# Pooled attention with two MLPs: products with v of two key tiles in one TensorE task, in all pairs of heads

## The chip, the cores and the metric

The kernel runs on one core of one Trainium2 chip. The metric is the device time of one execution in microseconds (us), the median of several runs. TensorE is called PE here, VectorE DVE, ScalarE ACT, GpSimd POOL, and SyncE, whose queue issues all DMAs of this kernel, SP.

## What is computed

```python
# q, k, v: (2, 8, 1152, 64); 16 heads in all
q_pool = q.reshape(B, H, S // 2, 2, D).mean(axis=3)        # 576 pooled queries a head
scores = (1 / sqrt(D)) * q_pool @ k.transpose(0, 1, 3, 2)  # 576 x 1152
attn = softmax(scores, axis=-1)
x = (attn @ v)  -> (1152 tokens, 512)
h = x @ moe_w_in;  x = maximum(0.01 * h, h) @ moe_w_out    # 512 -> 2048 -> 512
h = x @ moe2_w_in; out = (h * sigmoid(h)) @ moe2_w_out
```

## The kernel before, in words

**Tiling.** Attention works on 8 pairs of heads, one after the other, numbered p = 0 to 7. The two heads of a pair (j = 0, 1) share the partitions, 64 rows each. The keys lie in 9 tiles of 128 (t = 0 to 8). For each head and key tile, `scores` makes 128 keys x 576 queries in two halves of 288 columns: per half two matmuls at L675, the second one adding the low part of q and the negated row maximum, and then ACT takes the exponential at L679 into a tile `e` in SBUF. A ring holds ten such tiles, five key tiles of both heads. The row maxima of a pair are found one pair ahead: `max_tile` makes 27 groups a pair of scores on PE (L586; L582 and L583 for the rows left over), and DVE reduces each at L590. Scores and maxima take turns in six PSUM banks; two more banks belong to the product with v.

**The products.** `pv` (L701) multiplies the `e` tiles of a key tile with v. A step is four matmuls at L712: two halves of 288 columns, and in each the two heads, whose outputs lie on partitions 0 to 63 and 64 to 127. They stand in F32, so the trace shows two records for each matmul, 8 for a step. All 9 steps of a pair accumulate in the same two banks; ACT then copies these out (`evac_pv`, L727).

**The rest of a pair.** POOL adds the `e` tiles up over the keys (`sum_up`, L696, 16 adds a pair, on DVE in the last pair). When the 16th is done, PE sums them over the partitions (`sums`, L741), and small DMAs bring the reciprocals into shape (DVE L776). DVE and ACT scale and split the result (`finish`, L816 to L820). For a later pair, POOL pools q (L480), ACT and DVE split q and k into a high and a low part (L350, L499, L504), and DMAs on SP move these where PE wants them. In the later pairs, the first weights of the MLPs are loaded and split too, the low part on POOL (L169).

**What sets the order.** All work is put down as tasks of a `Plan`, each with an engine, a weight (its assumed time), a due time, what it comes after, and tokens that it takes and gives (banks, tiles). `Plan.run` goes through a model of time: an engine that is free takes the ready task with the earliest due time, and the instructions are written out in the order in which the tasks begin there. So the due time and the weight of one kind of task can move the instructions of all engines. On the chip each engine then works in the order written, and waits by semaphores. A `pv` task has the weight 0.25 + 0.98 for each key tile in it.

**The loop around the change.** For each pair, `attention` puts down the scores and exponentials of all key tiles, the adds, and then a task `pv` for each entry of a list of groups of key tiles; the task comes after all exponentials of its group, and is due by its last key tile. The list of groups for the last pair stands in `PARAMS`:

```python
    last_pv=((0, 1), (2, 3), (4, 5), (6, 7), (8,)),
```

The MLPs follow attention, with a plan of their own. Their lines are L1080 (first matrix), L1151 and L1200 (second).

Of the kernel before, what the change touches and what calls it, by code (L numbers as in the profile page):

```python
# [18 lines left out]
def pooled_attention_two_mlps(  # L19
# [27 lines left out]
    t=26.5,  # L47
# [10 lines left out]
    last_pv=((0, 1), (2, 3), (4, 5), (6, 7), (8,)),  # L58
# [227 lines left out]
def attention(ctx, tc, q, k, v, xh, xl, weights, end_p):  # L286
# [4 lines left out]
    NKT = S // 128  # L291
# [4 lines left out]
    NP = B * H // 2  # L296
# [7 lines left out]
    P = PARAMS  # L304
# [101 lines left out]
    def load_v(p, due):  # L406
        b, h0 = p // HP, 2 * (p % HP)

        def go():
            vnat[p] = nat.tile([128, 2, NKT, D], F32, tag="vnat", name="vnat")  # L410
            return vnat[p], v[b, h0:h0 + 2].rearrange("j (p t) d -> p j t d", p=128)

        return dma(due, go, take=("vnat",), lag=6.0, begin=due)
# [139 lines left out]
    def copy_ka(p, j, out, due, after):  # L553
        if p == 0:
            parts = (slice(0, 512), slice(512, S))
            for i, cs in enumerate(parts):
                go = lambda cs=cs: (KA[p % 2, j][own[j], cs].bitcast(F32), K2[p, j][own[j], cs].bitcast(F32))
                out["ka", j, i] = [dma(due, go, after=out["kh", j, i] + after, lag=3.0)]
        else:
            go = lambda: (KA[p % 2, j][own[j]].bitcast(F32), K2[p, j][own[j]].bitcast(F32))  # L560
            out["ka", j, 0] = out["ka", j, 1] = [dma(due, go, after=out["kh", j, 0] + after, lag=P["lag"] + 1.0)]
# [34 lines left out]
    def max_unit(u2, out, due, after):  # L596

        p = 0
        j, u = divmod(u2, NFULL + 1)
        deps = []  # L600
        for i in (0, 1) if u == NFULL else (j,):
            deps += out["qu", i][0 if u < 2 else 1] + out["k", i, 0] + out["k", i, 1]

        def pe():
            i = box["trio", u2] = trios.pop(0)
            ps = psum[:, i:i + 3].rearrange("p b n -> p (b n)")
            for c in range(0, S, 512):
                ks = slice(c, min(c + 512, S))
                for h, cs, rows in ((1, slice(SQ - 128, SQ), 128), (0, slice(NFC, SQ), HALF)) if u == NFULL else ((j, slice(u * 128, (u + 1) * 128), 128),):
                    nc.tensor.matmul(out=ps[0:rows, ks], lhsT=QH[p, h][:, cs], rhs=K2[p, h][:, ks], start=True, stop=True)  # L610

        def dve():
            i = box.pop(("trio", u2))
            ps = psum[:, i:i + 3].rearrange("p b n -> p (b n)")
            nc.vector.tensor_reduce(out=max_row(p, j)[:, u:u + 1], in_=ps[:, 0:S], op=ALU.max, axis=AX.X, negate=True)
            (trios.append if u2 < 2 * NFULL - 1 else lambda i: banks.extend(range(i, i + 3)))(i)

        t = add("PE", 1.05 if u == NFULL else 0.53, due, pe, after=deps, take=("trio",))
        t = add("DVE", 1.37, due - 1.0, dve, after=[t], give=("trio",) if u2 < 2 * NFULL - 1 else ("bank",) * 3)
        finish_rows(p, j, [u], t, out, due, after)  # L620
# [224 lines left out]
    for p in range(NP):  # L845
        at = lambda x: T0 + (p + x) * T
        out = {}
        due = 0.0 if p == 0 else P["load1"] if p == 1 else at(P["load"])
        loads = load_kq(p, due, due)
        value = load_v(p, at(-0.6) if p else P["load0"])  # L850
        if p == 0:
            for j in range(2):
                prep_first(p, j, loads, out)
        else:
            prep(p, loads, P["prep1"] if p == 1 else [at(x) for x in P["prep"]], out)
        for j in range(2):
            copy_ka(p, j, out, at(-0.5) if p else 5.0 + 2 * j, scored.get((p - 2, j), []) + (filled[p] if p < 2 else []))
        maxima = {}
        for u in range(2 * NFULL + 1 if p == 0 else 0):
            max_unit(u, out, 1.0 + 1.4 * u, filled[0])  # L860
        for n in range(NM if p else 0):
            lo, hi = P["max"]
            due = at(lo + (hi - lo) * n / NM)
            j, u = n // NA, n % NA // NCH
            maxima.setdefault((j, u), []).append(max_tile(p, n, out, due))
        for j in range(2 if p else 0):
            after = scored.get((p - 3, j), []) + (filled[p] if p < 3 else [])
            us = list(range(NFULL + 1 - j))
            finish_max(p, j, us, sum((maxima[j, u] for u in us), []), out, at(-0.2), after)
        ex, av = {}, {}  # L870
        steps = [(t, j) for t in range(NKT) for j in range(2)]
        if p == 0:
            steps = [(t, 0) for t in range(P["lead"])]
            for t in range(NKT):
                steps += [(t, 1)] + [(t + P["lead"], 0)] * (t + P["lead"] < NKT)
        for i, (t, j) in enumerate(steps):
            due = at(i / (2 * NKT))
            ex[t, j], before = scores(p, t, j, out, due, before)
            if t == 1:
                av[t, j] = sum_up(p, t, j, ex[0, j] + ex[1, j], [av[1, 0]] if j else [], due + 2.0)  # L880
            elif t > 1:
                av[t, j] = sum_up(p, t, j, ex[t, j] + [av[t - 1, j]], [], due + 2.0)
        if p == 0:
            add("-", 0.0, 0.0, after=[x for t in range(P["lead"]) for x in ex[t, 0]], give=("v",))
        last = []
        for ts in P["last_pv"] if p == NP - 1 else [(t,) for t in range(NKT)]:
            after = [x for t in ts for j in range(2) for x in ex[t, j]] + ([] if ts[0] else [value])
            x = pv(p, ts, at((2 * ts[-1] + 1) / (2 * NKT)) + P["pv"], after, last)
            last = [x]
            for t in ts:  # L890
                for j in range(2):
                    add("-", 0.0, 0.0, lambda t=t, j=j, p=p: e_t.pop((p, j, t)), after=[x, av[max(t, 1), j]], give=(("e", p, t, j),))
        for j in range(2):
            scored[p, j] = ex[NKT - 1, j]
        add("-", 0.0, 0.0, after=scored[p, 0] + scored[p, 1], give=("ops",))
        values = evac_pv(p, last[0], at(1.0) + 1.0)
        ends = [av[NKT - 1, 0], av[NKT - 1, 1]]
        if p < NP - 1:
            finish(p, sums(p, ends, at(P["sums"])) + values, at(P["norm"] + 0.3 * (p == NP - 2)))
# [396 lines left out]
```

## Time and profile before

| | |
|---|---|
| median of 3 runs | 666.66 us (666.63 to 666.75) |
| span of the profiled execution, first to last instruction | 664.7 us |
| its own time | not listed apart; the median of the runs lies 2.0 us above the span |
| PE busy | 646.1 us, 97% of the span |
| POOL busy, DVE busy, ACT busy | 392.0, 441.3, 326.8 us |
| attention (up to the first L1080 matmul) | 259.4 us |

A busy share is a mean over stages. Matmuls are pipelined and the records of two neighbours overlap, so what a matmul costs is read from one start to the next start, not from its length. Where an engine waits, the row says so in brackets, with the engine that released it.

### The profile page before, as it was taken

The numbers are of one execution on the slowest core, as the hardware profiler recorded it, in microseconds if no ns is written. First come the engines' busy times: TensorE is split into PE (matmuls) and PEld (weight loads), VectorE is DVE, ScalarE is ACT, GpSimd is POOL, SyncE is SP. The second block draws the span as 40 slices with busy tenths as digits, with TensorE's granted clock in tenths as the row PEclk, the third lists the DMA queues.
The fourth block names the chain that finished last, engine by engine and source line by source line (L and its number), as shares of the span: only waits on it lengthen the run. The fifth ranks groups of instructions, "written<-read, shape, count | busy, mean of one in ns | idle before, by whom it ended". The sixth has DMA issues, their size and how long they took to land.

```text
span 664.7 us, 9922 instructions
## 1 busy us (share of the span) xinstructions
PE 646.1 (97%) x3616; PEld 534.6 (80%) x3616; DVE 441.3 (66%) x614; ACT 326.8 (49%) x661; POOL 392.0 (59%) x278
## 2 busy tenths in 40 slices
PE   4889999999999998999999999999999999999997
PEld 3666777777777766988988988999988998888986
DVE  7284756678878766875676676698988888522222
ACT  4655766758686566554533433355456534312110
POOL 8657888897999833644544544476656453522120
PEclk9789999999999999999999999999999999999999
DMA  8636455455944130132233223232233322000012
GB/s 213 139 107 149 126 152 145 116 163 136 263 120 135 52 97 19 63 101 92 94 95 96 96 96 95 96 96 76 83 96 128 103 88 96 0 1 1 0 48 95
DMA packets 27959, 65.87 MB, mean 99 GB/s; under 512 B 9324, under 2 KB 9352, under 8 KB 27912
## 3 DMA queue, kind: packets, MB, share of 16 engines
q1 hardware_dynamic: 27912, 65.26, 33.7%
q8 instruction: 28, 0.46, 0.3%
q14 instruction: 19, 0.16, 0.1%
HBM read 49.81 MB, written 2.42 MB: 79 GB/s over the span
## 4 chain that ended last, share of the span: by engine, by line
PE 93%; POOL 2%; DMA 1%; ACT 1%; DVE 1%; issue 1%; SPq 0%; ACTq 0%; POOLq 0%; DVEq 0%
PE ph L1080 30%; PE po L1151 15%; PE pf L1200 15%; PE psum L675 12%; PE psum L712 11%; PE psum L586 7%; DMA k<-e 1%; PE psum L741 1%; DMA knat<-in_k_dram 1%; PE psum L583 1%; PE psum L582 1%; POOL k L439 0%; POOL e L504 0%; ACT qh L350 0%; ACT k L350 0%
## 5 line engine op out<-in xcount | busy, mean ns | idle before, releaser
L1133 POOL TENSOR_TENSOR gl<-a,gh 128x512 fp32r<-128x512 f32 (+1 forms) x64 | 97.3, 1520 | 143.1 <-ACT gh L1127 76.4
L696 POOL TENSOR_TENSOR acc<-acc,e 128x576 f32<-128x576 f32 x98 | 147.4, 1529 | 24.2 <-ACT e L679 23.8
L590 DVE TENSOR_REDUCE mx<-psum 128x1 f32<-128x384 f32 x189 | 96.5, 550 | 61.9 <-PE psum L586 55.7
L679 ACT ACTIVATE e<-psum 128x288 f32<-128x288 f32 x288 | 101.3, 414 | 69.8 <-PE psum L675 52.0
L1080 PE MATMUL ph<-xh,w0h 128*128 128x320 f32 (+1 forms) x384 | 109.0, 338 | 1.7 <-ACT pvs L727 1.7
L1080 PE MATMUL ph<-xl,w0h 128*128 128x320 f32 (+1 forms) x384 | 108.7, 337 | 0.0
L1080 PE MATMUL ph<-xh,w0l 128*128 128x320 f32 (+1 forms) x384 | 108.7, 337 | 0.0
L675 PE MATMUL psum<-qh,k 128*128 128x288 f32 x288 | 88.3, 323 | 1.7 <-ACT e L679 1.7
L712 PE MATMUL psum<-e,vnat 128*64 128x288 f32 x576 | 85.9, 423 | 0.0
L675 PE MATMUL psum<-ql,ka 128*128 128x288 f32 x288 | 81.8, 300 | 0.5 <-DMA ql<-mn 0.5
L675 PEld LDWEIGHTS psum<-qh,k 128*128 128x128 f32 x288 | 56.4, 196 | 26.3 <-issue 13.6
L1080 PEld LDWEIGHTS ph<-xh,w0h 128*128 128x128 f32 x384 | 67.7, 188 | 9.3 <-ACT pvs L727 2.2
L134 DVE TENSOR_SCALAR wt<-wt 128x512 f32<-128x512 f32 x56 | 40.3, 720 | 50.0 <-ACT wt L130 50.0
L1080 PEld LDWEIGHTS ph<-xh,w0l 128*128 128x128 f32 x384 | 66.9, 188 | 5.6
L1080 PEld LDWEIGHTS ph<-xl,w0h 128*128 128x128 f32 x384 | 66.9, 188 | 5.0
L169 POOL TENSOR_TENSOR w1l<-wt,w1h 128x512 fp32r<-128x512 f32 x32 | 44.4, 1398 | 39.1 <-ACT w1h L165 39.1
L586 PE MATMUL psum<-k,qh 128*128 128x384 f32 x168 | 62.8, 442 | 1.8 <-DMA k<-e 1.4
L169 POOL TENSOR_TENSOR w0l<-wt,w0h 128x512 fp32r<-128x512 f32 x32 | 44.7, 1396 | 24.3 <-ACT w0h L165 24.3
L138 DVE TENSOR_SCALAR wt<-wt 128x512 uint32<-128x512 uint32 x56 | 57.8, 1033 | 1.6
L712 PEld LDWEIGHTS psum<-e,vnat 128*64 128x64 f32 x576 | 35.8, 138 | 27.3 <-issue 12.0
L586 PEld LDWEIGHTS psum<-k,qh 128*128 128x128 f32 x168 | 47.1, 318 | 12.5 <-issue 4.9
L1106 ACT ACTIVATE gh<-ph 128x512 fp32r<-128x512 f32 (+1 forms) x32 | 20.9, 652 | 72.6 <-PE ph L1080 72.6
(89 smaller groups left out, 1162.8 us busy)
## 6 DMA issues: line engine op xcount, KB each, us to landing
wraw<-in_moe_w_in_dram SPq DMA_DIRECT2D x32, 512.0 KB, 3.9
wraw<-in_moe_w_out_dram SPq DMA_DIRECT2D x32, 512.0 KB, 3.3
vnat<-in_v_dram SPq DMA_DIRECT2D x8, 576.0 KB, 4.2
ka<-k SPq DMA_DIRECT2D x14, 288.0 KB, 5.2
knat<-in_k_dram SPq DMA_DIRECT2D x6, 576.0 KB, 6.0
qnat<-in_q_dram SPq DMA_DIRECT2D x6, 576.0 KB, 4.9
k<-knat SPq DMA_DIRECT2D x12, 288.0 KB, 3.3
out_dram<-acc SPq DMA_DIRECT2D x9, 256.0 KB, 2.0
```

The source lines that it names most:

```text
L138: nc.vector.tensor_scalar(out=t, in0=t, scalar1=4, scalar2=1, op0=ALU.logical_shift_left, op1=ALU.logical_shift_right)
L169: self.nc.gpsimd.tensor_tensor(out=lo, in0=tf, in1=hi, op=ALU.subtract)
L586: nc.tensor.matmul(out=ps[:, 0:KC], lhsT=QH[p, j][:, t:NFC:NFULL], rhs=K2[p, j][:, ks], start=True, stop=True)
L590: nc.vector.tensor_reduce(out=mx[p][:, n:n + 1], in_=ps[:, 0:KC], op=ALU.max, axis=AX.X)
L675: nc.tensor.matmul(out=ps[:, 0:C], lhsT=lhsT[:, ks], rhs=rhs[:, cs], start=not last, stop=last)
L679: nc.scalar.activation(out=e_t[p, j, t][:, cs], in_=ps[:, 0:C], func=ACTF.Exp, scale=scale)
L696: e.tensor_tensor(out=acc[p, j], in0=e_t[p, j, 0] if t == 1 else acc[p, j], in1=e_t[p, j, t], op=ALU.add)
L712: nc.tensor.matmul(out=vps[p, c][own[j], 0:C], lhsT=vnat[p][:, j, t, :], rhs=e_t[p, j, t][:, c * C:(c + 1) * C], start=(t == 0), stop=(t = ...
L1080: nc.tensor.matmul(out=box[x][:, c, 0:n], lhsT=wt[:, kk, fs], rhs=m[:, kk, chunk(g, c)], start=(kk == 0 and wt is wh and m is xh), stop=(k ...
L1133: nc.gpsimd.tensor_tensor(out=gl, in0=box["a", x], in1=gh, op=ALU.subtract)
L1151: nc.tensor.matmul(out=box[x][:, c, 0:n], lhsT=wt[:, f, ms], rhs=y[:, c * n:(c + 1) * n], start=(f == 0 and wt is oh and y is gh), stop=(f ...
L1200: nc.tensor.matmul(out=box[x][:, 0, :], lhsT=y[:, ts], rhs=wt[:, f, :], start=(f == 0 and y is gh and wt is oh), stop=(f == FB - 1 and y i ...
```

## The change

The groups of key tiles that the last pair had are used in all pairs. The first seven pairs had nine tasks `pv` of one key tile each; now they have four of two and one of one. Nothing else is edited. No instruction is added or taken away; since the order on every engine comes out of the plan, instructions move.

```diff
         last = []
-        for ts in P["last_pv"] if p == NP - 1 else [(t,) for t in range(NKT)]:
+        for ts in P["last_pv"]:
             after = [x for t in ts for j in range(2) for x in ex[t, j]] + ([] if ts[0] else [value])
             x = pv(p, ts, at((2 * ts[-1] + 1) / (2 * NKT)) + P["pv"], after, last)
```

Three places in the order of instructions follow. A count x4 at L712 is one step of `pv`, x8 two steps; four rows at L675 in a row are the scores of one head with one key tile.

PE where pair 1 goes over into pair 2, before: the scores at L675 with `qh_205` and `qh_207` are the last ones of pair 1, L586 the first row maxima for pair 3.

```order
L712 MATMUL psum<-e,vnat 64x288 x4
L675 MATMUL psum<-qh_205,k_204 128x288
L675 MATMUL psum<-ql_100,ka_98 128x288
L675 MATMUL psum<-qh_205,k_204 128x288
L675 MATMUL psum<-ql_100,ka_98 128x288
L586 MATMUL psum<-k_570,qh_571 128x384 x2
L675 MATMUL psum<-qh_207,k_206 128x288
L675 MATMUL psum<-ql_105,ka_103 128x288
L675 MATMUL psum<-qh_207,k_206 128x288
L675 MATMUL psum<-ql_105,ka_103 128x288
L586 MATMUL psum<-k_570,qh_571 128x384 x2
L712 MATMUL psum<-e,vnat 64x288 x4
```

The same place of the change; `qh_336` and `qh_338` are the first scores of pair 2.

```order
L586 MATMUL psum<-k_568,qh_569 128x384 x2
L712 MATMUL psum<-e,vnat 64x288 x8
L586 MATMUL psum<-k_568,qh_569 128x384 x2
L675 MATMUL psum<-qh_336,k_335 128x288
L675 MATMUL psum<-ql_101,ka_97 128x288
L586 MATMUL psum<-k_568,qh_569 128x384 x2
L675 MATMUL psum<-qh_338,k_337 128x288
L675 MATMUL psum<-ql_106,ka_102 128x288
L675 MATMUL psum<-qh_338,k_337 128x288
L675 MATMUL psum<-ql_106,ka_102 128x288
L586 MATMUL psum<-k_568,qh_569 128x384
L712 MATMUL psum<-e,vnat 64x288 x4
```

The steps for key tiles 6 and 7 stand together, half a score of pair 2 stands ahead of them, and the first maxima for pair 3 begin there and no longer two score tiles earlier.

PE in pair 0, as one piece of the difference: L586, L582 and L583 are the row maxima for pair 1, the first of which wait for a DMA.

```order
 L675 MATMUL psum<-qh_114,k_113 128x288
 L675 MATMUL psum<-ql_104,ka_102 128x288
-L586 MATMUL psum<-k_204,qh_205 128x384 x7
-L712 MATMUL psum<-e,vnat 64x288 x4
-L586 MATMUL psum<-k_204,qh_205 128x384 x5
+L712 MATMUL psum<-e,vnat 64x288 x8
+L586 MATMUL psum<-k_204,qh_205 128x384 x12
 L582 MATMUL psum<-k_206,qh_207 128x384
 L583 MATMUL psum<-k_204,qh_205 64x384
```

The third step of `pv` of the pair, which stood among the maxima, is gone from there; it now stands in the task for key tiles 2 and 3, behind the maxima.

POOL from the pooling of q (L480) in pair 4's last adds to the first adds of pair 6, before: `acc<-e` begins the sums of a pair, L169 is the low part of a piece of weights.

```order
L480 TENSOR_TENSOR qnat<-qnat 128x576
L696 TENSOR_TENSOR acc<-e 128x576
L169 TENSOR_TENSOR w0l<-wt,w0h 128x512
L696 TENSOR_TENSOR acc<-e 128x576
L696 TENSOR_TENSOR acc<-acc,e 128x576 x7
L169 TENSOR_TENSOR w0l<-wt,w0h 128x512
L696 TENSOR_TENSOR acc<-acc,e 128x576 x6
L169 TENSOR_TENSOR w0l<-wt,w0h 128x512
L696 TENSOR_TENSOR acc<-acc,e 128x576
L696 TENSOR_TENSOR acc<-e 128x576 x2
```

The same place of the change.

```order
L480 TENSOR_TENSOR qnat<-qnat 128x576
L696 TENSOR_TENSOR acc<-e 128x576 x2
L696 TENSOR_TENSOR acc<-acc,e 128x576 x2
L169 TENSOR_TENSOR w0l<-wt,w0h 128x512
L696 TENSOR_TENSOR acc<-acc,e 128x576 x8
L169 TENSOR_TENSOR w0l<-wt,w0h 128x512
L696 TENSOR_TENSOR acc<-acc,e 128x576 x4
L696 TENSOR_TENSOR acc<-e 128x576
L169 TENSOR_TENSOR w0l<-wt,w0h 128x512
```

Between this L480 and the 16th add of pair 5 there were three pieces of weights, and now there are two; the third comes behind the first add of pair 6. On POOL nothing else moves.

## Rows read from the trace of the kernel before

**Rows 1.** The page: busy time and share of engines, then the chain that ended last.

```profile
PE 646.1 (97%) x3616; PEld 534.6 (80%) x3616; DVE 441.3 (66%) x614; ACT 326.8 (49%) x661; POOL 392.0 (59%) x278
...
PE 93%; POOL 2%; DMA 1%; ACT 1%; DVE 1%; issue 1%; SPq 0%; ACTq 0%; POOLq 0%; DVEq 0%
```

**Rows 2.** Two stretches of one pair each: length, then busy time of each engine (instructions).

```profile
69.68:99.18 29.50, 29.50 (x183) 21.43 (x182) 19.76 (x35) 19.79 (x47) 25.40 (x18) 1.00 0.47 131
99.18:128.69 29.51, 29.51 (x183) 21.42 (x183) 19.75 (x35) 19.79 (x47) 25.41 (x18) 1.00 0.48 132
```

**Rows 3.** Timeline of PE in pair 2: start, length, line, tile, records.

```profile
111.38 0.29 PE L675 MATMUL psum<-ql,ka 128*128 128x288 f32 x1
111.60 1.19 PE L712 MATMUL psum<-e,vnat 128*64 128x288 f32 x8
112.72 0.40 PE L675 MATMUL psum<-qh,k 128*128 128x288 f32 x1
112.96 0.29 PE L675 MATMUL psum<-ql,ka 128*128 128x288 f32 x1
```

**Rows 4.** Timeline of PE in pair 7, which has products of two key tiles.

```profile
243.43 0.40 PE L675 MATMUL psum<-qh,k 128*128 128x288 f32 x1
...
245.80 0.29 PE L675 MATMUL psum<-ql,ka 128*128 128x288 f32 x1
246.03 2.16 PE L712 MATMUL psum<-e,vnat 128*64 128x288 f32 x16
248.12 0.41 PE L675 MATMUL psum<-qh,k 128*128 128x288 f32 x1
248.36 0.30 PE L675 MATMUL psum<-ql,ka 128*128 128x288 f32 x1
```

**Rows 5.** Timeline of PE in pair 0, around the maxima for pair 1.

```profile
34.79 1.74 PE L586 MATMUL psum<-k,qh 128*128 128x384 f32 x6 [1.41 <-DMA k<-e]
36.46 2.19 PE L712 MATMUL psum<-e,vnat 128*64 128x288 f32 x8
...
43.18 0.40 PE L675 MATMUL psum<-qh,k 128*128 128x288 f32 x1
```

**Rows 6.** Timeline of DVE in the same stretch.

```profile
35.47 2.88 DVE L590 TENSOR_REDUCE mx<-psum 128x1 f32<-128x384 f32 x6 [1.42 <-PE psum L586]
39.32 7.06 DVE L590 TENSOR_REDUCE mx<-psum 128x1 f32<-128x384 f32 x15 [0.98 <-PE psum L586]
```

**Rows 7.** Two stretches of pair 0, columns as in rows 2; 1.00 and 0.50 are the granted clock.

```profile
36.49:39.90 3.41, 3.41 (x13) 2.08 (x13) 2.43 (x7) 1.69 (x3) 2.77 (x2) 0.50 0.17 62
39.90:50.00 10.10, 9.72 (x45) 7.28 (x44) 10.06 (x19) 6.78 (x12) 5.13 (x3) 1.00 0.27 57
```

**Rows 8.** Timeline of POOL from pair 2 to pair 5.

```profile
110.92 10.73 POOL L696 TENSOR_TENSOR acc<-acc,e 128x576 f32<-128x576 f32 x7 [0.51 <-ACT e L679]
...
181.94 1.42 POOL L480 TENSOR_TENSOR qnat<-qnat 128x576 f32<-128x576 f32 x1
...
209.10 1.27 POOL L169 TENSOR_TENSOR w0l<-wt,w0h 128x512 fp32r<-128x512 f32 x1
210.33 1.93 POOL L696 TENSOR_TENSOR acc<-acc,e 128x576 f32<-128x576 f32 x1
```

**Rows 9.** Timeline of PE: the sums over the partitions of pairs 2, 4 and 5.

```profile
122.89 0.69 PE L741 MATMUL psum<-acc,ones 128*32 128x288 f32 x8
...
183.64 0.69 PE L741 MATMUL psum<-acc,ones 128*32 128x288 f32 x8
...
214.66 0.69 PE L741 MATMUL psum<-acc,ones 128*32 128x288 f32 x8
```

**Rows 10.** Timeline of DVE at the end of pair 7, where POOL has no work.

```profile
256.24 0.75 DVE L816 TENSOR_TENSOR pvs<-pvs,r 128x576 f32<-128x576 f32 x1
```

**Rows 11.** The page's groups: POOL's adds and the exponentials, busy us and mean ns.

```profile
L696 POOL TENSOR_TENSOR acc<-acc,e 128x576 f32<-128x576 f32 x98 | 147.4, 1529 | 24.2 <-ACT e L679 23.8
L679 ACT ACTIVATE e<-psum 128x288 f32<-128x288 f32 x288 | 101.3, 414 | 69.8 <-PE psum L675 52.0
```

## The prediction

> **What bounds the kernel now.** The page comes first. PE is busy for 97% of the span, and the chain that ended last lies on PE for 93% of it [rows 1]. So time saved on PE counts, wherever PE does not run into another wait. That is asked of the stretch that the change touches, attention up to 259 us: the windows of one pair each show PE busy for all of its 29.50 us, DVE and ACT for 19.8 each, POOL for 25.40 [rows 2]. POOL is the next engine, with 4.1 us of air. The busy share alone doesn't prove that PE never stands still, since the records overlap; so the starts in the timeline are read. Score matmuls follow each other every 0.13 us: 18 start from 243.43 to 245.80, the first distance 0.24, behind a product, and the other 16 together 2.13 [rows 4].
>
> **What a product costs.** One step of `pv`, alone between scores: from the start of the last score matmul to the product 0.22, from there to the next score 1.12, from that to the one behind it 0.24, in all 1.58 us [rows 3]. Without the product these would be two distances of 0.13. So it adds 1.58 - 0.26 = 1.32. The last pair has products of two steps: 0.23 + 2.09 + 0.24 = 2.56, less 0.26, so 2.30 [rows 4]. Two apart cost 2.64, two together 2.30: **0.34 us for each merge**. About 0.15 of it lies inside the task (2 x 1.12 - 2.09), 0.20 in the slower step from scores into products and back, which falls away once. These are the same instructions at the same clock as those that are merged, so I take this price as it stands.
>
> **The sum, part by part.** Seven pairs get four merges each, 28 in all.
>
> Pairs 1 to 6: 24 merges, 24 x 0.34 = 8.2 us. A pair would take 29.50 - 1.36 = 28.14 us.
>
> Pair 0, tiles 0 and 1: both steps stood ahead of the row maxima for pair 1, which begin at 34.79 after 1.41 us of waiting for a DMA [rows 5]. They still stand ahead of them. The chain of that DMA runs over POOL and SP, whose order up to there is unchanged. The wait grows by what the merge saves: 0.
>
> Pair 0, tiles 2 and 3: the step for tile 2 stood among the maxima, at 36.46 to 38.58 [rows 5]. There PE isn't the limit: DVE reduces a group every 0.47 us (15 in 7.06), and PE runs six banks ahead at most. The step cost DVE a wait of 0.98 us [rows 6], so PE's next scores at 43.18 came about that much later. Now this goes, and the step costs 2.30 - 1.32 = 0.98 behind the maxima. Net 0.
>
> Pair 0, the other two merges: 2 x 0.34 = 0.7 us.
>
> The order around the merged tasks. Each stands behind the exponentials of both its tiles. In the order at least 1.0 us of scores and maxima stands between the last score that a task needs and the task itself; an exponential takes 0.41 a half [rows 11] and ends within that, as long as ACT isn't behind. The `e` tiles are held longer by one key tile at most, out of five in the ring. The score tiles behind a merged task come in longer runs, four tiles and a half where two stood. The last pair already has such a run, nine halves (18 matmuls) in 2.6 us [rows 4], and shows no widened start in it. That is other where maxima follow at once and want banks too; a wait there would cost about one exponential less what PE does meanwhile, some 0.3 us a pair, 1.8 in all. I take 0 and keep 1.8 for the range. The maxima for the pair after next begin two score tiles later, and end behind tile 5 as before; up to the next pair's scores that need them come seven score tiles (0.53 each) and two merged tasks, over 8 us, for one short reduction on DVE and one small DMA; free.
>
> POOL. In pairs 1 to 3 its work is unchanged, 25.4 us against a pair of 28.14. After the last five key tiles it lags: seven adds take 10.73 and end at 121.65, and PE's sum of that pair starts at 122.89, 1.24 later [rows 8, 9]. In the change I walk down the order from the start of the last score of tile 5. POOL first ends the other head's add, 1.5 later, then the seven, 10.73: 12.2. PE has ten score tiles at 0.53, ten maxima at 0.29 (six in 1.74 [rows 5]) and the products of tiles 4 to 8, 2 x 2.30 + 1.32, ahead of its sum: 14.1. Free. Pair 5 is tight. There POOL went from 181.94 to 210.33 + 1.93 = 212.26, 30.3 us, with three pieces of weights of 1.27; PE's sum came 2.4 later, and 31.0 after the sum of pair 4 [rows 8, 9]. Now two pieces stand there: 29.0. PE comes from sum to sum in 28.1. POOL began this stretch 1.7 ahead of PE's sum (181.94 against 183.64); 1.7 + 28.1 - 29.0 leaves 0.8, and a wait of POOL for an exponential in the new order can eat it. From below 0, from above about 1.5 if POOL waits as it did in the steady pairs; I take 0.4, nearer to 0, since 0.8 is there.
>
> DVE and ACT keep 8 us of air a pair. The last pair and the MLPs stand in their old order: 0.
>
> Sum: -8.2 - 0.7 + 0.4 = -8.5. The profiled span of 664.7 becomes 656.2; with the 2.0 us by which the median lies above it, **658.2 us**.
>
> **The rivals.**
>
> *POOL takes over in every pair.* If an add slows PE's sum in each of the pairs 1 to 6 by 0.5 us, about 3 us go, and 661.2 is left. For it: POOL's 25.4 of 28.14 is 90%, and it waited 4.1 us a pair for exponentials, of which only 2.7 are left. Against it: these waits came from PE's pace and shrink with it. If all of them stayed, a pair would still take 25.4 + 4.1 = 29.5 us, and nothing would be won: 666. A rule of the Trainium skill ("SBUF — State Buffer", section "Who interferes with whom") speaks for this rival: a DVE instruction with two inputs in SBUF and a GpSimd instruction that reads SBUF exclude each other for the whole length of one. The trace bears it out in part: the mean add takes 1.53 us and one takes 1.93 [rows 8, 11]. As an estimate by that page, with all of them apart: 17 POOL instructions at 1.42 and the DVE ones of a pair at 0.75 for 576 columns [rows 10], five such lengths, give 24.1 + 3.75 = 27.9, just under 28.14; the steady pairs would not change by it, and pair 5 would, by up to 2 us.
>
> *Slower than before: the adds get longer.* If POOL's adds meet DVE's instructions more often in the new order, POOL sets the pace from the point where 16 adds, one pooling of 1.42 and some 1.3 of waits exceed a pair of before plus what can be told: (29.7 - 2.7) / 16 = 1.69 us an add, against a mean of 1.53 [rows 11]. At the longest seen, 1.93, a pair takes 33.6, and six pairs add 24: 691 us. Against it: DVE's instructions are the same ones, and the mean would have to rise by a tenth.
>
> *The clock.* PE reaches the DMA wait of pair 0 earlier and stands longer. A stretch at 0.50, 1.2 GHz, followed this wait at 36.49 to 39.90, and 1.00 after it [rows 7]; a step took 2.12 there [rows 5] against 1.12. If this came to lie over the two steps of tiles 2 and 3, it costs 2 us: 660.2.
>
> *The merge doesn't do what it says*, since the waits only move: each task waits for an exponential that single steps didn't meet. With 0.34 a merge this needs the same wait at each, and gives 666.
>
> **How the numbers follow.** The forecast 658.2, with its own range of 656.9 to 659.5, has 0.70. POOL in every pair: 0.14, to 662. The clock: 0.06, at 660.2. No change that counts (POOL keeps its old pace, or the waits move): 0.05. Slower: 0.05. Within 0.2%, 1.3 us, is about what a measurement of this kernel can't tell from no change. So faster 0.90, same 0.05, slower 0.05. The range reaches up through the clock and most of POOL's case, 656.8 to 661.2; the rest of POOL's, no change and slower leave out about 0.18.
>
> **What would show it.** Right: L712 records in groups of 16, 2.09 us to the next start; windows of a pair of 28.1 us with PE busy throughout; attention ending near 251 us; the MLPs as long as before. In pair 5 a gap of at most a few tenths ahead of PE's sum, released by POOL. Wrong: PE idle ahead of the sums, released by POOL's adds, in each pair; starts of more than 0.13 apart in the runs of scores ahead of the maxima; adds with a mean above 1.6; a stretch at 0.50 after 40 us. The number falls with the price of 0.34 if scores that stand together now are slowed by something that the single steps hid.

## The result, and the profile after

The change takes 661.13 us (median of 4 runs, 660.69 to 662.79), the kernel before 666.7 beside it: a ratio of 0.992, 95% interval 0.9906 to 0.9934. Four runs more of the change gave 661.17. So it gains some 5.5 us, where 8.5 were forecast, and ends above the forecast's own range of 656.9 to 659.5. The profiled run of the change is its longest, 662.79, with a span of 661.0; a second profile of the same kernel, called e12 below, has a span of 659.9.

From the page of the change: busy time of the engines, the chain that ended last by engine, and POOL's adds [rows 1, 11].

```profile
PE 641.0 (97%) x3616; PEld 538.4 (81%) x3616; DVE 441.5 (67%) x614; ACT 325.5 (49%) x661; POOL 390.6 (59%) x278
...
PE 90%; DMA 2%; DVE 2%; POOL 2%; ACT 1%; issue 1%; SPq 0%; DVEq 0%; ACTq 0%; POOLq 0%
...
L696 POOL TENSOR_TENSOR acc<-acc,e 128x576 f32<-128x576 f32 x98 | 145.7, 1514 | 20.8 <-ACT e L679 20.6
```

PE carries 90% of the chain where it carried 93%; DMA and DVE have come in with 2% each. POOL's adds are no longer than before, 1514 ns against 1529.

A merged product in pair 2 of the change, in PE's timeline [rows 3, 4]:

```profile
103.78 2.16 PE L712 MATMUL psum<-e,vnat 128*64 128x288 f32 x16
105.87 0.40 PE L675 MATMUL psum<-qh,k 128*128 128x288 f32 x1
106.10 0.29 PE L675 MATMUL psum<-ql,ka 128*128 128x288 f32 x1
```

2.09 to the next start and 0.23 behind it, as in the last pair before. Now from sum to sum, the windows of pairs 1 to 5 of the change (columns as in rows 2):

```profile
64.58:92.84 28.26, 28.26 (x184) 21.84 (x183) 19.54 (x34) 19.55 (x47) 26.32 (x18) 1.00 0.51 137
92.84:121.04 28.20, 28.20 (x183) 21.77 (x182) 19.23 (x34) 19.47 (x48) 24.97 (x18) 1.00 0.54 138
121.04:149.30 28.26, 28.26 (x184) 21.83 (x183) 19.13 (x34) 19.48 (x48) 25.06 (x18) 1.00 0.62 155
149.30:178.86 29.56, 29.39 (x189) 22.52 (x188) 23.19 (x41) 21.71 (x52) 26.33 (x20) 1.00 0.70 181
178.86:209.08 30.22, 29.41 (x181) 21.79 (x180) 25.70 (x43) 21.56 (x50) 27.39 (x19) 1.00 0.47 129
```

The steady pairs take 28.2 to 28.3 us, as forecast (28.14). Where the weights of the MLPs are loaded and converted, from 149 us on, PE has gaps that it did not have. Three marks of PE's timeline cut attention into parts with the same work: the sums of pairs 0 and 3, and the first product of the MLPs. Before the change:

```profile
63.88 0.69 PE L741 MATMUL psum<-acc,ones 128*32 128x288 f32 x8
...
152.40 0.69 PE L741 MATMUL psum<-acc,ones 128*32 128x288 f32 x8
...
259.36 0.50 PE L1080 MATMUL ph<-xh,w0h 128*128 128x512 f32 x1 [1.67 <-ACT pvs L727]
```

The change, in e12:

```profile
64.56 0.69 PE L741 MATMUL psum<-acc,ones 128*32 128x288 f32 x8
...
149.19 0.69 PE L741 MATMUL psum<-acc,ones 128*32 128x288 f32 x8
...
254.59 0.50 PE L1080 MATMUL ph<-xh,w0h 128*128 128x512 f32 x1 [1.62 <-ACT pvs L727]
```

| part | before | change (e12) | gain | forecast |
|---|---|---|---|---|
| start to sum of pair 0 | 63.88 | 64.56 | -0.7 | 0.7 |
| sum 0 to sum 3 | 88.52 | 84.63 | 3.9 | 4.1 |
| sum 3 to the MLPs | 106.96 | 105.40 | 1.6 | 3.7 |
| MLPs (to the end of the span) | 405.3 | 405.3 | 0.0 | 0 |

The middle is right, pair 0 and the pairs with weights are not. In the first profile (marks at 64.58, 149.30 and 255.72) the third row is worse still, 106.42; what its extra 1.0 us is stands under e6. The first row sets one profile against one, and it moves by about 1 us from run to run, as shown under e12.

### The profile page after: what moved, and what is told of

It is laid out like the page before. It is cut to its first block, busy times and chain, and to the rows that moved or that the text cites. A ratio compares the mean times of both kernels' runs of the same rounds, so it can differ in the third digit from the quotient of the medians.

```text
span 661.0 us, 9906 instructions
## 1 busy us (share of the span) xinstructions
PE 641.0 (97%) x3616; PEld 538.4 (81%) x3616; DVE 441.5 (67%) x614; ACT 325.5 (49%) x661; POOL 390.6 (59%) x278
## 4 chain that ended last, share of the span: by engine, by line
PE 90%; DMA 2%; DVE 2%; POOL 2%; ACT 1%; issue 1%; SPq 0%; DVEq 0%; ACTq 0%; POOLq 0%
PE ph L1080 31%; PE po L1151 15%; PE pf L1200 15%; PE psum L675 11%; PE psum L712 10%; PE psum L586 7%; DMA k<-e 1%; DMA cmp<-d 1%; PE psum L741 1%; DMA qnat<-in_q_dram 1%; DVE mx L590 1%; PE psum L582 1%; PE psum L583 0%; ACT qh L350 0%; SPq L345 0%
## 5 line engine op out<-in xcount | busy, mean ns | idle before, releaser
L696 POOL TENSOR_TENSOR acc<-acc,e 128x576 f32<-128x576 f32 x98 | 145.7, 1514 | 20.8 <-ACT e L679 20.6
L679 ACT ACTIVATE e<-psum 128x288 f32<-128x288 f32 x288 | 99.2, 420 | 56.7 <-PE psum L675 50.2
L675 PE MATMUL psum<-qh,k 128*128 128x288 f32 x288 | 86.4, 318 | 2.1 <-ACT e L679 1.4
L675 PE MATMUL psum<-ql,ka 128*128 128x288 f32 x288 | 82.2, 302 | 0.0
L712 PE MATMUL psum<-e,vnat 128*64 128x288 f32 x576 | 79.2, 416 | 0.0
L675 PEld LDWEIGHTS psum<-qh,k 128*128 128x128 f32 x288 | 57.0, 198 | 16.3 <-issue 10.1
L586 PE MATMUL psum<-k,qh 128*128 128x384 f32 x168 | 64.2, 452 | 3.7 <-DMA k<-e 2.6
L169 POOL TENSOR_TENSOR w1l<-wt,w1h 128x512 fp32r<-128x512 f32 x32 | 44.4, 1397 | 38.5 <-ACT w1h L165 38.5
L712 PEld LDWEIGHTS psum<-e,vnat 128*64 128x64 f32 x576 | 38.2, 138 | 28.2 <-issue 7.8
L169 POOL TENSOR_TENSOR w0l<-wt,w0h 128x512 fp32r<-128x512 f32 x32 | 45.2, 1412 | 25.8 <-ACT w0h L165 25.8
L586 PEld LDWEIGHTS psum<-k,qh 128*128 128x128 f32 x168 | 47.8, 318 | 14.6 <-issue 7.1
```

The source lines that it names most:

```text
L169: self.nc.gpsimd.tensor_tensor(out=lo, in0=tf, in1=hi, op=ALU.subtract)
L586: nc.tensor.matmul(out=ps[:, 0:KC], lhsT=QH[p, j][:, t:NFC:NFULL], rhs=K2[p, j][:, ks], start=True, stop=True)
L675: nc.tensor.matmul(out=ps[:, 0:C], lhsT=lhsT[:, ks], rhs=rhs[:, cs], start=not last, stop=last)
L679: nc.scalar.activation(out=e_t[p, j, t][:, cs], in_=ps[:, 0:C], func=ACTF.Exp, scale=scale)
L696: e.tensor_tensor(out=acc[p, j], in0=e_t[p, j, 0] if t == 1 else acc[p, j], in1=e_t[p, j, t], op=ALU.add)
L712: nc.tensor.matmul(out=vps[p, c][own[j], 0:C], lhsT=vnat[p][:, j, t, :], rhs=e_t[p, j, t][:, c * C:(c + 1) * C], start=(t == 0), stop=(t = ...
```

## The experiments

Each was timed in five rounds beside the kernel before, which took 666.4 to 666.9 in these comparisons. Lines are those of the change unless an added line moves them.

**e1 and e2: which pairs give the gain.** The condition in the loop over `P["last_pv"]` keeps single products in pair 0 (e1) or in pairs 4 to 6 (e2).

```
-        for ts in P["last_pv"]:
+        for ts in P["last_pv"] if p > 0 else [(t,) for t in range(NKT)]:                  # e1
+        for ts in P["last_pv"] if p < 4 or p == NP - 1 else [(t,) for t in range(NKT)]:   # e2
```

> The change, but with single products in pair 0. Leading theory: the change lost some 1.5 us in pair 0 (its first merged task behind the maxima lies open, since ACT's copies hold the exponentials until 43.6 us, and part of it runs at the low clock); then this kernel is 1 to 2 us faster than the change, about 659.5, ratio 0.989. Rival (pair 0 is neutral or gains, as predicted, and the loss is all in later pairs): the same as the change or up to 0.7 us slower, 661 to 662, ratio 0.992 to 0.993.

> Merged products in pairs 0 to 3 and 7, single ones in pairs 4 to 6, where the first weights are converted. Leading theory: DVE's queue in pairs 4 to 6 gives back about 3.5 us of the 4.1 that twelve merges are worth there; then this kernel is about as fast as the change, within 1 us, 661 to 662, ratio 0.992 to 0.993. Rival (a merge is worth less than 0.34 everywhere, say 0.22, also in pairs 4 to 6): 2.5 us or more slower than the change, 664 or above, ratio 0.996 or above.

e1 took 661.3 (0.9919, 0.9905 to 0.9932), the same as the change: the merges of pair 0 are worth nothing that can be told, neither a loss nor the 0.7 of the forecast. The profiles of all runs can't tell it either: the sum of pair 0 starts at 63.6 to 64.7 us in the seven with single products there, and at 63.4 to 64.7 in the thirteen with merged ones. e2 took 663.5 (0.9952, 0.9939 to 0.9964), between its two expectations: the twelve merges of pairs 4 to 6 give 2.4 us of 4.1.

What goes against the gain in pair 0 can be seen in the first profile of the change, here PE's timeline:

```profile
42.10 0.40 PE L675 MATMUL psum<-qh,k 128*128 128x288 f32 x1
...
43.84 0.80 PE L586 MATMUL psum<-k,qh 128*128 128x384 f32 x2 [0.74 <-ACT e L679]
```

and ACT's:

```profile
39.95 1.17 ACT L350 ACTIVATE kf<-knat 128x1152 fp32r<-128x1152 f32 x1
41.02 2.33 ACT L350 ACTIVATE k<-knat 64x1152 fp32r<-64x1152 f32 x2
43.38 0.71 ACT L679 ACTIVATE e<-psum 128x288 f32<-128x288 f32 x2
```

The scores come at 42.10, 1.08 earlier than before [rows 5], as forecast. But ACT copies keys until 43.4 and takes the exponentials only then; PE runs out of banks and waits 0.74. Most of the 0.98 us that I counted as won ahead of the merged task goes there. No experiment moved ACT's copies, so this is read from the trace alone.

**e4 and e5: the load of the conversions on DVE.** Three of the four DVE steps of a conversion in the attention (clamp, shift, sign) are left out, so that the weights are wrong numbers; e4 is the change, e5 the kernel before.

```
         def clamp():
+            if psum:
+                return
             tf = box["tf"]
```

> The change, without three of the four DVE steps of each of the eight weight conversions inside attention (clamp, shift, sign; the weights are then not the reference's); the order of everything else is the same. Theory that DVE's load holds PE in pairs 4 to 6: PE's new waits there fall from about 3.7 us to under 1, 658 or so. Theory that it is the reciprocal waiting in DVE's queue for a small DMA: about 1.3 us of them stay, since that DMA still stands behind a weight load, 659 to 660. Rival (the waits come from neither): no change, 661.

> The kernel before, without the same three DVE steps of each of the eight conversions. All theories: the same as before within 0.5 us, 666.2 to 666.7, since PE hardly waits in pairs 4 to 6 of before; if it were faster by over 1 us, DVE held PE there already and the comparison with the run above is to be read by the difference of the two.

e4: 660.83 (0.9913, 0.9899 to 0.9927), e5: 666.87. 24 steps of 0.69 us less on DVE change nothing beyond 0.3 us. The theory of DVE's load fell.

**e6: the reciprocal that waits for a small DMA.** In the first profile DVE stands 1.48 us at the reciprocal of pair 4's sums until `cmp<-d` lands, with maxima queued behind it.

```
-        x = add("DVE", 0.21, due, lambda: nc.vector.reciprocal(out=box["cmp", p], in_=box["cmp", p]), after=[x])
+        x = add("DVE", 0.21, due, inverse, after=[x])      # reciprocal of a tile of ones into a spare tile
```

> The change, but the reciprocal of the sums of a pair is taken of a tile of ones into a spare tile, so that it leaves out the inversion of the softmax sums and DVE never waits for the small DMA that brings them (cmp<-d). The order on every engine stays. Theory one (in pair 5 DVE stands 1.48 us at that reciprocal, the maxima behind it come late, and PE runs out of PSUM banks for about 1.3 us): 661.1 falls to about 659.9 (659.6 to 660.2), and the wait of 0.48 us on DVE's maxima at 193 us is gone. Rival (PE would have stood there anyway, because the longer runs of scores and maxima need more banks than there are): 660.9 to 661.3.

660.85 (0.992, 0.9907 to 0.9934): the rival's time. The wait is gone and PE stands all the same, from 191 us on; this theory fell too. The second profile of the change, e12, says the same: there the reciprocal waits too, 1.17 us, and from sum 3 to the MLPs e12 takes 105.40 us, e6 105.45. What made the first profile 1.0 us longer stands behind the wait. DVE's timeline, first profile:

```profile
190.31 0.22 DVE L776 RECIPROCAL cmp<-cmp 128x9 f32<-128x9 f32 x1 [1.48 <-DMA cmp<-d]
190.49 2.46 DVE L504 TENSOR_TENSOR knat<-knat,kf 128x1152 fp32r<-128x1152 f32 x1
```

and e12:

```profile
189.91 0.22 DVE L776 RECIPROCAL cmp<-cmp 128x9 f32<-128x9 f32 x1 [1.17 <-DMA cmp<-d]
190.09 1.39 DVE L504 TENSOR_TENSOR knat<-knat,kf 128x1152 fp32r<-128x1152 f32 x1
```

PE's timeline, first profile:

```profile
193.47 0.40 PE L675 MATMUL psum<-qh,k 128*128 128x288 f32 x1 [0.48 <-DVE mx L590]
```

The same instruction at L504, two inputs in SBUF, took 2.46 us in one run and 1.39 in the other, in both beside a row of POOL's adds; the maxima behind the longer one came late, and PE waited for them. A second such wait, 0.27 us, stands at 208.3 us, behind L820 (1.98 us, in e12 0.92). In e12 PE has neither. Why the same instruction took longer in one run was not tested.

**e7 to e11: the conversion's bank.** e7 is e4 with the conversion worked out in SBUF, so that it holds no PSUM bank; e8 adds e6's edit, e9 is e7's edit in the kernel before. e10 is e7 with only the conversion's first step, on ACT, left; e11 adds e6's edit to e10. All leave the named steps out, and the weights are wrong numbers.

```
-            box["tf"] = psum() if psum else t.bitcast(F32)
+            box["tf"] = t.bitcast(F32)
...
-                    if m == 4:
-                        banks.append(box.pop(("conv", i))[1])
         def tail():
+            if psum:
+                return                                     # e10, e11
```

> The kernel of e4 (the change without three of the four DVE steps of each weight conversion in the attention), and in addition the conversions work in SBUF, so that they hold no PSUM bank between their first step on ACT and their last on DVE; the orders stay, and the converted weights are wrong numbers as in e4. Theory two (in pairs 4 to 6 a conversion holds one of the six banks, so that the longer runs of scores and maxima wait for a bank, 0.3 to 0.6 us each time at 164, 177, 200, 208 and 217 us): e4's 660.8 falls by about 1.5 to 659.3 (659.0 to 659.7). Rival (the bank is not what is short): 660.6 to 661.0.

> Both edits, e6's and e7's, with what each leaves out. Theories one and two both: about 2.5 us under e4's 660.8, 658.2 (657.9 to 658.7), which is the forecast for the change. One of them alone: as e6 or e7 alone. Neither: 660.6 to 661.0.

> The kernel before with the edits of e7 (leaves out the same steps). Its PE had almost no stall in pairs 4 to 6 (0.9 us in all), so theory two and the rival both expect 666.4 to 667.0, the time before; a fall by more than 0.5 us would say that banks were short there already, and that e7's gain is no part of what the change met.

e7 took 662.27 (0.9942, 0.9928 to 0.9955), 1.4 more than e4, e8 662.65, e9 666.6. Slower was nobody's expectation. Groups of lines between 150 and 236 us, first e4:

```profile
L153 DVE SCALAR_TENSOR_TENSOR wt<-wraw,psum 128x512 uint32<-128x512 uint32 x8 | 5.4, 681 | 0.9 <-ACT psum L130 0.9
...
L702 POOL TENSOR_TENSOR acc<-acc,e 128x576 f32<-128x576 f32 x42 | 62.4, 1514 | 6.2 <-ACT e L685 6.2
```

then e7:

```profile
L153 DVE SCALAR_TENSOR_TENSOR wt<-wraw,wt 128x512 uint32<-128x512 uint32 x8 | 10.1, 1265 | 0.6 <-ACT wt L130 0.6
...
L702 POOL TENSOR_TENSOR acc<-acc,e 128x576 f32<-128x576 f32 x42 | 65.7, 1593 | 4.7 <-ACT e L685 4.7
```

and PE's timeline of e7 at the sum of pair 6:

```profile
235.59 0.69 PE L747 MATMUL psum<-acc,ones 128*32 128x288 f32 x6 [1.20 <-POOL acc L702]
```

The step that now reads two tiles of SBUF takes 1.27 instead of 0.68 us and POOL's adds get 0.08 longer, 3.3 us in 42; the sum of pair 6 waits 1.2 for POOL. That is the forecast's POOL rival at one sum, made by the experiment. The rule cited there (the Trainium skill, "SBUF — State Buffer", "Who interferes with whom") agrees with these rows. So e7's time gave no verdict on the bank. e10 takes that step away as well.

> e7 without the DVE step that it still had (a conversion in the attention is now its first step on ACT alone, into SBUF; the later steps are left out, and the weights are wrong numbers). In e7 that step read and wrote SBUF alone and took 1.27 us, where e4's took 0.68, POOL's additions took 1.59 instead of 1.51, and the sum of pair 6 waited 1.2 us for POOL, which hid what the bank was worth. The orders stay. Theory two (a conversion that holds a PSUM bank makes PE wait after the longer runs: 0.2, 0.3, 0.34, 0.2 and 0.34 us at five places in e4 and e6): e4's 660.8 falls by 1.4 to 659.4 (659.0 to 659.9), and no stall over 0.2 us is left in the pairs 4 to 6 but the one at 199 us. Rival (the bank is not short, what e7 lost is something else): 660.5 to 661.1.

> e10 with e6's reciprocal of a tile of ones (leaves out the inversion of the softmax sums too). If the reciprocal's wait costs what e6 showed, 0.3 to 0.5 us: 0.3 to 0.5 under e10, about 659.0. If with a bank more PE has cover enough for late maxima, the same as e10 within 0.3.

e10: 659.88 (0.9898, 0.9885 to 0.9912), 0.95 under e4 and 1.3 under the change; e11: 659.38 (0.989, 0.9876 to 0.9903). The same place in PE's timelines shows what went, in the change (the rows behind a single product):

```profile
176.78 0.30 PE L675 MATMUL psum<-qh,k 128*128 128x288 f32 x1
176.92 0.29 PE L675 MATMUL psum<-ql,ka 128*128 128x288 f32 x1
177.36 0.40 PE L675 MATMUL psum<-qh,k 128*128 128x288 f32 x1
```

and in e10:

```profile
176.53 0.30 PE L683 MATMUL psum<-qh,k 128*128 128x288 f32 x1
176.68 0.29 PE L683 MATMUL psum<-ql,ka 128*128 128x288 f32 x1
176.80 0.30 PE L683 MATMUL psum<-qh,k 128*128 128x288 f32 x1
```

0.44 between two scores became 0.12. The gaps of 0.2 to 0.35 us at 164, 177, 192 and 216 us (times of e12) are all gone, the one at 199 and the wait in the sum of pair 6 are not. From sum 3 to the MLPs e10 takes 104.1, 1.3 less than e12. Theory two held, at 1.0 to 1.3 instead of 1.4. In e10 the fourth DVE step went together with the bank; e7's trace parts the two, since there the step is left, and longer. The same place in e7:

```profile
175.87 0.29 PE L681 MATMUL psum<-ql,ka 128*128 128x288 f32 x1
176.05 0.40 PE L681 MATMUL psum<-qh,k 128*128 128x288 f32 x1
```

0.18 between the two, and the other three gaps are gone in e7 as well. e4, which holds the bank and has the same DVE steps, has them all. So at these four places it is the bank. e11 adds nothing to e10: from sum 3 to the MLPs both take 104.1 us. That its median is 0.5 lower lies in pair 0, whose sum starts at 64.69 us in e10's profile and at 63.40 in e11's.

**e3 and e12: the other half, and the change again.** e3 merges in the pairs 4 to 7 alone (`if p > 3` in e1's line).

> Products of two tiles in one task in the pairs 4 to 6 and the last alone (12 merges more than before, none in the pairs 0 to 3). Theory two (what the weights' conversions take back depends on the merges of these pairs): 12 x 0.34 = 4.1 less some 1.7, so 664.3 (663.9 to 664.7), and with e2's 663.5 the two halves add up to the whole change, 3.2 + 2.4 = 5.6. Rival (the merges of the pairs 0 to 3 moved the planner's order in the later ones, and that took 1.7): 662.6 (662.2 to 663.0).

> The change itself once more, for a firmer time beside e10 and e11, since its first four runs lay 2.1 us apart: 661.1 (660.7 to 661.6). Theory three (the clock falls to 0.50 for 3.4 us at a different moment of pair 0 in each run, 37.8 and 44.7 us in the first profile): the profile of this run has its sum of pair 0 between 63.5 and 64.6 us, with a 0.50 stretch elsewhere, and that is what sets the runs apart; the rival is a difference spread over the span.

e3: 666.37 (0.9994, 0.9985 to 1.0003). Neither theory had that: the merges of pairs 4 to 6 by themselves gain 0.3 us, those of pairs 0 to 3 gain 3.2 (e2), and both 5.5. What a merge there is worth depends on where the plan puts everything else. In e3 two causes can be seen: the sum of pair 5 takes 1.50 us instead of 0.69, with a piece of weights on POOL ahead of its last add, and maxima come late behind conversions, in PE's timeline:

```profile
197.93 0.57 PE L586 MATMUL psum<-k,qh 128*128 128x384 f32 x1 [0.65 <-DVE mx L590]
```


For theory three, windows of pair 0; the column ahead of the last two is the granted clock [rows 7]. First e12:

```profile
34.43:37.84 3.41, 3.11 (x10) 3.05 (x10) 2.29 (x5) 0.00 (x0) 1.24 (x1) 0.50 0.74 272
...
44.66:48.08 3.42, 3.42 (x15) 2.58 (x16) 3.22 (x5) 1.23 (x3) 2.71 (x2) 0.57 0.01 2
```

then e11:

```profile
34.43:37.84 3.41, 3.41 (x11) 3.19 (x11) 2.61 (x6) 0.00 (x0) 1.41 (x2) 0.54 0.67 251
...
44.66:48.08 3.42, 3.40 (x24) 2.12 (x22) 3.07 (x5) 1.20 (x3) 3.18 (x2) 1.00 0.08 20
```

e12 has the second stretch at nearly the same place as the first profile; that its moment differs in each run, as theory three had it, did not hold there. Among the thirteen profiles with merged products in pair 0, three (the first one, e10, e12) have this second stretch at 0.50, 1.2 GHz, for 3.4 us from 44.2 to 44.7 us on, behind the wait for ACT; the other ten, e11 among them, have 1.00 there. e11's PE waited for ACT as well, 0.88 us, so that wait alone does not bring it. The sums of pair 0 start at 64.6 to 64.7 in the three, at 63.4 to 63.9 in the ten. So a run with the second stretch is about 1 us longer. That may be why e12's four runs lie at 660.3, 660.7, 661.7 and 662.0; runs without a profile can't show it. It does not belong to the merged products: e3, with single ones in pair 0, has a clock of 0.50 from 43.94 to 47.35 us, and its sum starts at 64.47.

**e13 and e14: the order that the plan's price makes.** The plan reckons a product at 0.25 + 0.98 for each tile, and by that places the weights' tasks, which have times of their own, among the others. The price moves more than these: PE's order differs from 31 us on in e13 (against before) and from 75 us on in e14 (against the change). e13 is the kernel before with its single products priced at half of a merged one; e14 is the change with merged products priced at two single ones. No work is added or removed.

```
-        w = 0.25 + 0.98 * len(ts)
+        w = 0.25 + 0.98 * len(ts) if p == NP - 1 else 1.105 if ts[0] < 8 else 1.23    # e13
+        w = 0.25 + 0.98 * len(ts) if p == NP - 1 else 1.23 * len(ts)                  # e14
```

> The kernel before, single products, but the plan reckons a product of one tile at 1.105 instead of 1.23, so that a pair takes as long in the plan as in the change and the weights' loads and conversions, which have times of their own in the plan, fall at the places among the attention's tasks at which they fall in the change, as near as single tasks allow. No work is added or removed. Theory four (this move of the order by itself costs PE some 1 us in the pairs 4 to 6; e2, whose products there are those of before, lost 0.9 us there): 667.6 (667.1 to 668.2). Rival (the order alone costs nothing, only merged products run out of banks): 666.4 to 667.0.

> The change, but the plan reckons a product of two tiles at 2.46 instead of 2.21, twice the single one, so that the weights' loads and conversions stand among the attention's tasks about where they stand before the change. No work is added or removed. Theory four: 660.2 (659.7 to 660.6), and the small stalls of the pairs 4 to 6 shrink by about 1 us. Theory two alone (merged products run out of banks beside conversions wherever these stand): 660.9 to 661.6.

e13: 670.72 (1.0052, 1.004 to 1.0065), 3.8 slower than before from the order alone, beyond both expectations. By the marks it loses 1.3 us between the sums of pairs 0 and 3, and 3.2 from there to the MLPs. The timeline of e13, ACT and PE:

```profile
156.14 0.62 ACT L130 ACTIVATE psum<-wraw 128x512 f32<-128x512 f32 x1 [3.06 <-DMA wraw<-in_moe_w_in_dram]
156.69 0.48 ACT L748 ACTIVATE sum<-psum,tiny 128x288 f32<-128x288 f32 x1
...
157.23 0.40 PE L675 MATMUL psum<-qh,k 128*128 128x288 f32 x1 [1.69 <-ACT sum L748]
```

The first conversion now stands on ACT before its weights have landed; the sum and the exponentials queue behind it for 3.06 us, and PE waits 1.69 for ACT. e14: 664.64 (0.9968, 0.9956 to 0.998), 3.5 slower than the change, against the expectation. Against e12 it loses 2.2 us between the sums of pairs 0 and 3, 0.8 of it in pair 1 already, where nothing is converted, and 1.4 from there to the MLPs. ACT's timeline in pair 1 of e14:

```profile
70.54 1.17 ACT L350 ACTIVATE kf<-knat 128x1152 fp32r<-128x1152 f32 x1
71.61 1.15 ACT L350 ACTIVATE k<-knat 64x1152 fp32r<-64x1152 f32 x1
72.66 1.72 ACT L679 ACTIVATE e<-psum 128x288 f32<-128x288 f32 x5
```

and PE's:

```profile
73.11 0.56 PE L586 MATMUL psum<-k,qh 128*128 128x384 f32 x1 [0.36 <-ACT e L679]
```

Two copies in a row hold ACT for 2.1 us while PE sends it scores, the same thing as in pair 0 of the change. So theory four fell, as a rule that before's prices are better and in its size of some 1 us. What the two runs show is that another order alone, with the same work, cost 3.8 and 3.5 us.

**e15: another order of the weights.** `weights_due=1.5` instead of 1.0.

> The change with weights_due 1.5 instead of 1.0: the steps of a conversion are due half a pair later and give way to maxima, and the small DMA cmp<-d of pair 5 is issued ahead of a weight load again. No work is added or removed. Theory two: a conversion's bank is held over 22 maxima instead of 18 in all, so no gain from banks; 660.9 to 661.7. Theory four (any other order of these tasks moves the stalls): anything between 660.2 and 662.0, with the stalls at other places than 177, 192, 199, 216 and 235 us.

662.45 (660.69 to 662.83; 0.9927, 0.9914 to 0.9939): no better than the change, and just outside the range given. From sum 3 to the MLPs its profile takes 105.4 us, as e12's.

**e16 and e17: e3 and e2 without the conversions' bank and DVE steps** (e10's edit, with what it leaves out).

> e3 (two-tile products in the pairs 4 to 6 and the last alone) with e10's conversions (their first step on ACT alone, into SBUF; the later steps are left out, and the weights are wrong numbers). Theory two and e10 (the bank and the DVE steps of the conversions are what eats the merges of these pairs): e3's 666.4 falls by 2 or more, to 663.5 to 664.5. Rival (the order that the plan makes is what eats them, conversions or not): 665.5 to 666.4.

> e2 (two-tile products in the pairs 0 to 3 and the last) with the same conversions, which leave out the same steps. Single products in the pairs 4 to 6 run out of banks less: theory two expects at most 0.9 less than e2's 663.5, the time that e2 lost there against the kernel before, so 662.6 to 663.3. Then with e16 the two halves (some 4.0 and 2.6) add up to the 6.8 that e10 gained. Rival: 663.3 to 663.8, and the halves still do not add up.

e16: 665.45 (0.9985, 0.9976 to 0.9994); e17: 661.76 (0.993, 0.9918 to 0.9943). e16 came out at its rival's time, e17 below both of its expectations, and the two halves, 1.0 and 4.7, do not add up to e10's 6.8. Side by side, gains against the kernel before as it is (with e10's edit it was not run; with e7's, e9, it took the same time):

| merges in pairs | conversions as they are | first step on ACT alone | forecast |
|---|---|---|---|
| 0 to 3 (e2, e17) | 3.2 | 4.7 | 4.8 |
| 4 to 6 (e3, e16) | 0.3 | 1.0 | 3.7 |
| all (change, e10) | 5.5 | 6.8 | 8.5 |

That e17's 4.7 is so near to the 4.8 of the forecast is luck. By the marks of its profile 3.9 us of the gain lie in pairs 1 to 3, as in e12. Another 0.5 lies in pair 0, where the start of the sum moves by 1 us with the same merges, and 0.4 in pairs 4 to 6, which have no new merges. What e17 shows is the way of the conversions: from sum 3 to the MLPs e2 takes 107.9 us, e17 106.5, before 107.0. The merges of pairs 0 to 3 had moved the order of the later pairs into the conversions' way, at 0.9 us against before, and that is gone. The second half stays poor, and one cause is plain in e16. PE's timeline at the sum of pair 5:

```profile
212.31 0.69 PE L749 MATMUL psum<-acc,ones 128*32 128x288 f32 x6 [0.79 <-POOL acc L704]
```

and POOL's:

```profile
209.63 1.28 POOL L177 TENSOR_TENSOR w0l<-wt,w0h 128x512 fp32r<-128x512 f32 x1
210.87 1.39 POOL L704 TENSOR_TENSOR acc<-acc,e 128x576 f32<-128x576 f32 x1
```

A piece of the weights stands on POOL ahead of the last add, and PE waits for it: the wait of 0.4 that was forecast for pair 5, twice as long. In the change itself the sum of pair 5 does not wait for POOL. The sum of pair 6 does, inside its eight matmuls; PE and POOL in e12:

```profile
234.53 1.03 PE L741 MATMUL psum<-acc,ones 128*32 128x288 f32 x8
...
221.33 13.49 POOL L696 TENSOR_TENSOR acc<-acc,e 128x576 f32<-128x576 f32 x9 [1.63 <-ACT e L679]
```

POOL's last add of the pair ends at 234.82, and the sum takes 1.03 us instead of 0.69.

**e18: a repair.** The four DVE steps of a conversion as one task, nothing left out.

```
-            steps = weights.convert_steps(psum)
+            begin_step, *rest = weights.convert_steps(psum)
+            steps = (begin_step, lambda rest=rest: [f() for f in rest])
```

> The change with the four DVE steps of a weight conversion in one task, so that no maximum stands between them and its PSUM bank is held for the shortest time; nothing is left out. Theory two alone: up to 1 us faster than the change, 660.1 to 660.8. Rival (the maxima that come 2.75 us later behind such a block hold banks themselves): 661.3 to 663, with waits on DVE's maxima of 0.5 us and more.

670.07 (667.68 to 670.47; 1.0055, 1.0041 to 1.0068), slower than the rival gave. PE's timeline of e18:

```profile
179.74 0.69 PE L741 MATMUL psum<-acc,ones 128*32 128x288 f32 x8 [1.77 <-DVE wt L147]
```

A block of 2.8 us on DVE costs PE 1.0 to 1.8 us at a time, at 180, 206 and 214 us. The plan also moved the order of PE, ACT and POOL from about 180 us on, so not all of the loss need be the block's. Still, a conversion's bank matters less here than maxima that come late. No version with the whole computation beat the change.

## Why the prediction was off

Of 8.5 us forecast some 5.5 came. The 3.0 that are missing lie, by the marks and by e1, at 0.7 in pair 0, 0.2 to 0.3 in pairs 1 to 3 and 2.1 in pairs 4 to 6.

- **Right: the price.** 0.34 us a merge. In pairs 1 to 3 twelve merges gave 3.8 to 3.9 us of 4.1, and a pair took 28.2 us.
- **Wrong: "Net 0" for tiles 2 and 3 of pair 0, and 0.7 for its other merges.** e1 measured about 0 for the four. The scores did come a microsecond earlier, but into ACT's copies of keys, and PE waited there. I had looked at DVE's maxima and not at what ACT was doing at 42 us.
- **Partly: the clock rival.** A stretch at 1.2 GHz came over the merged task of tiles 2 and 3 in some profiles, and cost about 1 us instead of 2. Kernels with single products in pair 0 have such stretches too, so it is not a cost of the change.
- **Wrong, and the largest: "I take 0" for longer runs that want banks, and "DVE and ACT keep 8 us of air a pair" with 0 to pay.** Both were made from the last pair and the mean of pair 2. They held in pairs 1 to 3 (0.2 to 0.3 us in three pairs). From pair 4 on, where conversions take DVE, ACT and a bank, 1.6 us came of 3.7. Of the 2.1 that did not come, the bank that a conversion holds took 1.0 to 1.3 us (e10, and e7 at the same gaps). The 1.8 kept for the range was near the 2.1 that were lost; I had put it on the pairs evenly and added it nowhere.
- **POOL.** The forecast wait of 0.4 before pair 5's sum is not there in the change: in e12 POOL's last add ends at 207.44 us and PE, late itself, begins the sum at 207.97. The sum of pair 6, for which no wait was forecast, waits 0.3. POOL did not take over, and the adds did not lengthen. So it is chance that the measured 661.1 lies beside the 661.2 that the forecast gave for POOL in every pair.
- **Not seen at all:** merges change the plan's own times, and so where the weights' tasks stand in pairs 4 to 6. e2 shows it, whose products in these pairs are those of before: sum 3 to the MLPs takes 107.9 there, 0.9 more than before. How large such a shift can be, e13 and e14 show.

Open: of the 2.1 us missing between sum 3 and the MLPs, e10 gives 1.3 back. Of the rest, 0.8, the gap of 0.2 at 199 us and the wait of 0.3 in the sum of pair 6 can be seen in the traces, but no experiment took them away. What of the loss a better order could save was not found: no order that was tried beat the change.

## What to carry to other kernels

A price per merge from a clean stretch holds only in stretches like it: list the stretches where another job shares the queues, and price the change in each one by itself. Mean air of an engine did not cover this: ACT was busy for half of the span and DVE for two thirds. What counted was the longest row of work in an engine's queue against the buffers that PE can fill meanwhile; here PE had six banks, and rows of 2.1 to 2.3 us on ACT and 2.8 us on DVE made it wait. And where a planner reads a cost, changing that cost is a change of its own: run it alone, in both directions, before crediting the work saved.

## What was not expected of the hardware

One DVE instruction of 512 columns took 0.68 us with one operand in PSUM and 1.27 with both in SBUF beside POOL's adds (e4, e7). One of 1152 columns with both inputs in SBUF took 1.39 us in one run of the change and 2.46 in another. And the clock: kernels that are the same up to the end of pair 0 had a second stretch at 1.2 GHz there or had none, with about 1 us between them.
